# A gated linear recurrence with a SiLU feed-forward on one core: every engine's program order written anew, buffers in fixed rings, sine from the table set of SiLU

## The chip, the core and the metric

The kernel runs on one core of one Trainium2 chip. The metric is device time in microseconds (us). The kernel before took 656.92 us, the median of three runs (657.31, 653.33 and 656.92). The profile shown below is of one further execution, whose first-to-last-instruction span is 655.6 us.

## What is computed

Cut to what matters:

```python
B, H, S, D = 4, 8, 768, 48
mag = sqrt(a_re**2 + a_im**2); scale = minimum(mag, 0.999) / (mag + 1e-6)
a = scale * (a_re + 1j * a_im)                  # one complex gate per step and channel
for t in range(S):
    S_re, S_im = Re(a_t * S) + k_t v_t^T, Im(a_t * S)
    y_t = q_t . S_re
x = y.transpose(0, 2, 1, 3).reshape(3072, 384)
h = x @ w_in                                    # 384 x 2048
out = (h * sigmoid(h)) @ w_out                  # 2048 x 384
```

All is in 32-bit floats; the two weights arrive as 64-bit words and are turned into 32-bit floats on the chip.

## The kernel before, in words

The sequence of each of the four batch rows is cut into six chunks of 128 steps, which makes 24 tiles, n = 0 to 23. Two tiles are a pair p = n // 2, so there are 12 pairs. A tile of chunk c in row b needs the state that the tile four places earlier left.

**The recurrence of a tile.** The gates become a log-magnitude `l` and an angle `th` (squares, logarithm, exponential, arctangent on ScalarE, the arithmetic on VectorE). A matmul with a triangle of ones sums them over the 128 steps: `phases` (L453) and `sums` (L489). `turn` (L462) takes the angle down to one turn, `trig` (L473) takes sine and cosine, `decays` (L502) the exponentials, `rotated` (L530) makes the rotated keys and queries. They must stand transposed. For tiles 0 to 3 that is done by TensorE (`turned` L544, with the copies `placed` L575). From tile 4 on it is done by VectorE in 32 x 32 blocks (L566, the tile `sq`) and by twelve DMAs, six on SyncE's queue and six on GpSimd's (L571), which carry the blocks to their places in `T`. `weights` (L578) multiplies keys with queries (the tile `a`), VectorE masks the result (L595, the tile `w`), `output` (L598) makes `y`, `state` (L664) and `carried_on` (L703) the new state; from tile 6 on the state too is turned by VectorE and twelve small DMAs (L691, L699). ScalarE copies `y` to `xT` (L623, L627) and six small DMAs (L631) spread the last two heads.

**The feed-forward of a pair.** There are eight groups: `hidden` (L720) multiplies two 128-column blocks of `w_in` with the 256 tokens of `xT`, `silu` (L731) takes the activation on ScalarE into `g`, and `result` (L763) adds that group's part of the output. Pairs 0 and 1 use plain products (L773). Pairs 2 to 11 use seven products of half blocks for eight (L817), which need sums of `g` (`gs`, L760, VectorE) and sums of the weights (`wc`, L748). The last of the eight ends with a ScalarE copy, seven VectorE adds (L825, L829) and the store.

**The weights.** There are 28 blocks. `fetch` (L182) loads one, ScalarE takes the low words (`convert_low`, L224), VectorE the high words (L47, L49) and joins them (L56). `small` (L243) and `looked_at` (L255) reload all of the weights in 32 parts near the end of the program and look for values too small for this conversion; with the smallest decay of all tiles (L1062 to L1073) they make the value `weak`, which every engine loads before it branches around a slow spare path (L1075 and L1076). A tile of `small` takes a buffer of the gates `re` or `im`, two of each.

**Order.** Each engine works through its instructions in the order in which they are written. Up to pair 2 this order is a list of words (L1019 to L1043) that was written by hand, as in "h:0" for the next group of `hidden` of pair 0. From pair 3 on it is one string of marks, `usual` (L1048), that is repeated for each pair: the feed-forward of pair p - 1 is spread between the attention steps of pair p and the gates of pair p + 1. After the last attention step the looks at the weights (`look`, L884) are taken between the remaining groups. The code after these lists (L1057 on), among it the making of `weak`, is placed by the scheduler of the compiler. Buffers come from pools that hand out one of several buffers for each name. A sequence of ScalarE functions from different table sets needs a table load; the sets are natural logarithm with exponential, arctangent with sine, and SiLU. L300 is the explicit load of `table`; L305 is the line of `special`, at which the compiler adds loads of its own.

Of the kernel before, what the change touches and what calls it, by code (L numbers as in the profile page):

```python
# [11 lines left out]
F32 = mybir.dt.float32  # L12
# [45 lines left out]

@with_exitstack
def kernel(  # L60
# [44 lines left out]
    ld = fast.enter_context(tc.tile_pool(name="ld", bufs=2))  # L105
    pre = fast.enter_context(tc.tile_pool(name="pre", bufs=1))
    att = fast.enter_context(tc.tile_pool(name="att", bufs=2))
    moe = fast.enter_context(tc.tile_pool(name="moe", bufs=2))
    setup = ExitStack()
    su = setup.enter_context(tc.tile_pool(name="su", bufs=1))  # L110
    conversion = ExitStack()
    cv = conversion.enter_context(tc.tile_pool(name="cv", bufs=1, side="right"))
    later = {}
    startup_psum = ExitStack()
    p_m = fast.enter_context(tc.tile_pool(name="p_m", bufs=2, space=PSUM))
    p_h = fast.enter_context(tc.tile_pool(name="p_h", bufs=2, space=PSUM))
    p_o = startup_psum.enter_context(tc.tile_pool(name="p_o", bufs=4, space=PSUM))
# [20 lines left out]
    def load_a(p, queue=None):  # L138
        for name in ("re", "im"):
            A[p][name] = flat(pre.tile([C, 2, H, D], F32, tag=name, name=f"{name}{p}", bufs=2))  # L140
        for i in range(2):
            b, c = place(2 * p + i)
            for name, ap in (("re", a_re), ("im", a_im)):
                (queue or (nc.gpsimd if p == 0 and i and name == "re" else nc.sync)).dma_start(
                    out=cut(A[p][name], i).rearrange("p (h d) -> p h d", d=D),
                    in_=ap[b].rearrange("h (c p) d -> p c h d", p=C)[:, c])

    def load_x(n, names="kqv", queue=None):
        b, c = place(n)
        for name, ap in zip("kqv", (k, q, v)):  # L150
            if name not in names:
                continue
            if name == "v":

                X[n]["all v"] = ld.tile([C, DM + 64 - D], F32, tag="v", name=f"v{n}", bufs=4)
                nc.gpsimd.memset(X[n]["all v"][:, DM:], 0.0)
                X[n]["v"] = X[n]["all v"][:, 0:DM].rearrange("p (h d) -> p h d", d=D)
            else:
                X[n][name] = ld.tile([C, H, D], F32, tag=name, name=f"{name}{n}", bufs=2)
            (queue or nc.sync).dma_start(  # L160
                out=X[n][name], in_=ap[b].rearrange("h (c p) d -> p c h d", p=C)[:, c])
# [42 lines left out]
    def words(n):  # L204
        if n == len(fetched):
            fetch(1)
        dst, _, parts = blocks[n]
        return dst, fetched[n], parts[0][1].dtype != F32

    def convert_high(n):  # L210
        for _ in range(min(n, len(blocks) - len(highs))):
            dst, raw, does = words(len(highs))
            if does:
                high_part(nc, dst, raw[:, :, 1])
            highs.append(dst)

    def convert_low(n):

        for _ in range(n):
            dst, raw, does = words(len(lows))  # L220
            r = None
            if does:
                r = cv.tile([C, WC], I32, tag="wr", name="r", bufs=3)[:, 0:dst.shape[1]]
                nc.scalar.mul(r, raw[:, :, 0].bitcast(U32), 2.0 ** -29)  # L224
            lows.append(r)

    def convert(n):

        for _ in range(min(n, len(blocks) - len(done))):
            if len(done) == len(lows):  # L230
                convert_low(1)
            if len(done) == len(highs):
                convert_high(1)
            dst, r = highs[len(done)], lows[len(done)]
            if r is not None:
                joined(nc, dst, r)
            done.append(dst)

    def converted(which):
        while any(x[1] == which for x in blocks[len(done):]):  # L240
            convert(1)
# [32 lines left out]
    load_a(0)  # L274
# [10 lines left out]
    chained = []  # L285
    by_hand = []
    looks, looked = [], []

    def behind(ins, other):
        tc.add_manual_dep(ins.ins, other.ins.name, mybir.DependencyInfo(  # L290
            mybir.DependencyClass.NoSync, mybir.DependencyReason.DATA))

    def chain(ins):
        if chained and not by_hand:
            behind(ins, chained[-1])
        chained.append(ins)


    def table(of):
        chain(nc.scalar.preload_act_table_set({  # L300
            "exp": "natural_log_exp_and_others", "trig": "trig_and_small",
            "silu": "silu_and_others"}[of]))

    def special(out, in_, func, **kw):
        chain(nc.scalar.activation(out=out, in_=in_, func=func, **kw))  # L305


    def tiles(p, i):

        g = A[p]  # L310
        if "th" not in g:
            for x in ("s1", "s2", "mag"):
                g[x] = flat(pre.tile([C, 2, H, D], F32, tag="t3", name=f"{x}{p}", bufs=5))
            for x in ("l", "th"):
                pool = su if p == 1 else pre
                g[x] = flat(pool.tile([C, 2, H, D], F32, tag=x, name=f"{x}{p}"))
        names = ("re", "im", "s1", "s2", "mag", "l", "th")
        return (g[x] if i is None else cut(g[x], i) for x in names)
# [5 lines left out]
    def squares(p):  # L324
        re, im, s1, s2, _, _, th = tiles(p, None)
        special(s1, re, AF.Square)
        special(s2, im, AF.Square)
        special(th, re, AF.Abs)

    def gates_square(p):  # L330

        squares(p)
        magnitude(p)

    def magnitude(p):
        re, im, s1, s2, *_ = tiles(p, None)
# [3 lines left out]
    def gates_log(p):  # L340

        re, im, s1, s2, mag, *_ = tiles(p, None)
        special(s1, s1, AF.Ln)
        special(mag, s1, AF.Exp, scale=0.5)
        gates_excess(p)

    def gates_excess(p):
        re, im, s1, s2, *_ = tiles(p, None)
# [3 lines left out]

    def gates_inverse(p):

        re, im, s1, s2, mag, _, th = tiles(p, None)
        nc.vector.tensor_tensor(out=mag, in0=mag, in1=th, op=ALU.add)
        special(mag, mag, AF.Ln)
        special(mag, mag, AF.Exp, scale=-1.0)


    def early_square(i):
        re, im, s1, s2, _, _, th = tiles(0, i)
        special(s1, re, AF.Square)
# [5 lines left out]
    def early_log(i):  # L369

        re, im, s1, s2, mag, l, _ = tiles(0, i)
        special(s1, s1, AF.Ln)
        special(s2, s1, AF.Exp, scale=-0.5)
        nc.vector.tensor_scalar(out=l, in0=s1, scalar1=LN_CAP2, scalar2=0.5, op0=ALU.min,
                                op1=ALU.mult)

    def early_l(i):
        re, im, s1, s2, mag, l, th = tiles(0, i)
        special(s2, s2, AF.Ln, scale=1e-6, bias=one_b)
        nc.vector.tensor_tensor(out=l, in0=l, in1=s2, op=ALU.subtract)  # L380
        special(mag, s1, AF.Exp, scale=0.5)
        nc.vector.tensor_tensor(out=mag, in0=mag, in1=th, op=ALU.add)
        sums(i)

    def early_ratio(i):
        *_, mag, _, _ = tiles(0, i)
        special(mag, mag, AF.Ln)
        special(mag, mag, AF.Exp, scale=-1.0)
# [3 lines left out]
    def gates_l(p, i=None):  # L392

        re, im, s1, s2, mag, l, _ = tiles(p, i)
# [3 lines left out]
    def gates_ratio(p, i=None):  # L398

        re, im, s1, s2, mag, l, _ = tiles(p, i)  # L400
        nc.vector.tensor_tensor(out=mag, in0=mag, in1=im, op=ALU.mult)

    def gates_atan(p, i=None):
        re, im, s1, s2, mag, *_ = tiles(p, i)
        special(mag, mag, AF.Arctan)

    def gates_side(p, i=None):

        re, *_ = tiles(p, i)
# [3 lines left out]
    def gates_angle(p, i=None):  # L413

        re, im, s1, s2, r, l, th = tiles(p, i)
# [12 lines left out]
    def in_two(n, x):  # L428
# [3 lines left out]
        t = later["left"].tile([C, 2, DM], F32R, tag="part", name=f"{x}_parts{n}", bufs=2)  # L432
# [20 lines left out]
    def phases(n):  # L453
# [5 lines left out]
        if n >= STRAIGHT:  # L459
            turn(n)  # L460
# [12 lines left out]
    def trig(n):  # L473
# [8 lines left out]
        if n >= STRAIGHT:  # L482
            last_of(n)
# [5 lines left out]
    def sums(n):  # L489
# [7 lines left out]
        if not first:  # L497

            x["L"] = x["ek"]
            nc.vector.tensor_scalar(out=x["L"], in0=ps, scalar1=L_MIN, scalar2=None, op0=ALU.max)  # L500

    def decays(n):  # L502
# [6 lines left out]
        if not n < STRAIGHT:  # L509
            ends_of(n)  # L510
# [19 lines left out]
    def rotated(n, which="kq", hs=slice(None)):  # L530

        x = X[n]
        for w in which:
            if (w, "decayed") not in x:
                decayed(n, w)
# [8 lines left out]
    def turned(n, groups=range(4)):  # L544


# [3 lines left out]
        T = x["T"]  # L550
        if n < EARLY:
            for g in groups:
                w, hh = divmod(g, 2)
                ps = (p_o if n < 4 else p_m).tile([D2, HH, C], F32, tag="o" if n < 4 else "m",
                                                  name=f"tp{n}_{g}")
                for h in range(HH):
                    nc.tensor.transpose(
                        ps[:, h],
                        x["kq"[w] + "r"][:, hh * HH + h].rearrange("p c d -> p (c d)"), ident)
                x["T", g] = ps  # L560
                if n >= STRAIGHT:
                    placed(n, g)
        else:
            sq = later["left"].tile([C, NB, 2 * H, Q], F32, tag="sq", name=f"sq{n}", bufs=2)
            for i, w in enumerate("kq"):
                nc.vector.transpose(sq[:, :, ts(i, H)], x[w + "r"].rearrange(  # L566
# [668 lines left out]
```

## Time and profile before

| what | value |
|---|---|
| median of 3 runs | 656.92 us |
| span of the profiled execution | 655.6 us |
| TensorE matmul busy | 634.7 us, 97% of the span |
| VectorE busy | 468.4 us, 71% |
| ScalarE busy | 367.2 us, 56% |
| GpSimd busy | 213.8 us, 33% |
| mean granted TensorE clock | 0.994 |
| bytes moved by DMA | 73.28 MB |

TensorE appears as PE, VectorE as DVE, ScalarE as ACT, GpSimd as POOL, SyncE as SP. Busy time is the union of the instructions of an engine. A matmul of 32-bit floats appears as two records. One 12-record group of `h` takes 2.59 us from start to start, one 14-record group of `o` 2.28 us. From 161 us to 513 us the same pattern returns every 50.24 us, once for each pair.

### The profile page before, as it was taken

Reading aid. Unit: us, or ns where it says so; the run is one execution under the profiler, and the core shown is the slowest. Engines: PE = TensorE matmul, PEld = TensorE weight load, DVE = VectorE, ACT = ScalarE, POOL = GpSimd, SP = SyncE. Lnnn points to the kernel's source line nnn. Section 1 sums busy time; section 2 is a strip of 40 time slices with the busy share of each in tenths; the row PEclk is TensorE's granted clock in tenths of the full one; section 3 lists DMA queues with packets and bytes.
Section 4 is the critical chain, followed back from the end, with each engine's and each line's share of the span. In section 5 each row is a group of like instructions: output and inputs, shape, how many; then the busy total and the mean of one; then the engine's idle time right before and its main releaser. Section 6 shows DMA issues by size and latency. Waiting matters only on the chain.

```text
span 655.6 us, 11519 instructions
## 1 busy us (share of the span) xinstructions
PE 634.7 (97%) x4084; PEld 562.1 (86%) x4084; DVE 468.4 (71%) x1009; ACT 367.2 (56%) x537; POOL 213.8 (33%) x368
## 2 busy tenths in 40 slices
PE   5789999999999999999999999999999999998997
PEld 4668866777999999999999999999999999987997
DVE  5898379847975885885895894894894895864543
ACT  6798599796852852762762672672681681410110
POOL 7436000370342334334334334234244240140000
PEclk9899999999999999999999999999999999998999
DMA  9878465583393394394295296187187183678640
GB/s 168 173 189 171 113 178 126 117 134 86 47 153 49 61 146 62 56 139 73 47 141 79 41 135 91 35 122 109 31 125 110 32 116 56 201 160 226 204 141 27
DMA packets 183445, 73.28 MB, mean 112 GB/s; under 512 B 166224, under 2 KB 171816, under 8 KB 183384
## 3 DMA queue, kind: packets, MB, share of 16 engines
q1 hardware_dynamic: 168424, 50.79, 39.5%
q0 software_dynamic: 11648, 17.20, 17.1%
q10 hardware_dynamic: 3312, 4.52, 1.9%
q8 instruction: 33, 0.54, 0.4%
q14 instruction: 28, 0.23, 0.1%
HBM read 48.90 MB, written 4.79 MB: 82 GB/s over the span
## 4 chain that ended last, share of the span: by engine, by line
PE 80%; ACT 7%; DVE 5%; DMA 4%; SPq 2%; issue 1%; DVEq 0%; ACTq 0%
PE h L725 32%; PE o L817 27%; PE a L584 6%; PE y L614 3%; PE o L773 3%; PE y L617 3%; DMA raw<-in_moe_w_in_dram 2%; PE s L687 2%; ACT L305 2%; SPq L571 1%; PE phase L446 1%; ACT mag L305 1%; ACT s L305 1%; PE L L446 1%; DMA im<-in_a_im_dram 1%
## 5 line engine op out<-in xcount | busy, mean ns | idle before, releaser
L725 PE MATMUL h<-xT,w 128*128 128x256 f32 x1152 | 260.6, 380 | 0.0
L725 PEld LDWEIGHTS h<-xT,w 128*128 128x128 f32 x1152 | 216.4, 190 | 29.2
L305 ACT ACTIVATE g<-h 128x512 f32<-128x512 f32 x96 | 55.3, 596 | 140.3 <-PE h L725 133.2
L571 POOL DMA_DIRECT2D T<-sq x120 | 77.5, 653 | 71.9 <-issue 56.0
L517 POOL DMA_DIRECT2D dec<-ends x48 | 30.8, 648 | 154.9 <-DMA ends<-eq 154.9
L300 ACT ACT_TABLE_LOAD x62 | 79.5, 1283 | 2.0 <-PEq L1219 0.9
L817 PE MATMUL o<-w,gs 128*128 128x192 f32 x320 | 77.8, 326 | 0.0
L699 POOL DMA_DIRECT2D S<-ssq x84 | 45.8, 553 | 94.8 <-DVE ssq L691 56.5
L595 DVE TENSOR_TENSOR w<-a,upto_r 128x512 f32<-128x512 f32 x48 | 32.9, 687 | 53.5 <-PE a L584 53.5
L817 PE MATMUL o<-w,g 128*128 128x192 f32 x320 | 67.2, 332 | 0.0
L817 PE MATMUL o<-wc,gs 128*128 128x192 f32 x320 | 64.9, 326 | 0.0
L623 ACT COPY xT<-y 128x384 f32<-128x384 f32 x20 | 9.6, 478 | 98.1 <-PE y L617 98.1
L817 PEld LDWEIGHTS o<-w,g 128*128 128x128 f32 x320 | 54.0, 191 | 4.5 <-issue 2.0
L817 PEld LDWEIGHTS o<-w,gs 128*128 128x128 f32 x320 | 56.3, 190 | 0.0
L584 PEld LDWEIGHTS a<-T 96*128 96x128 f32 x384 | 49.4, 191 | 7.6 <-issue 3.5
L584 PE MATMUL a<-T 96*128 96x128 f32 x384 | 51.3, 276 | 3.7 <-DMA T<-sq 2.5
L817 PEld LDWEIGHTS o<-wc,gs 128*128 128x128 f32 x320 | 54.2, 190 | 0.0
L760 DVE TENSOR_TENSOR gs<-g 128x128 f32<-128x128 f32 x160 | 38.6, 283 | 20.4 <-PE o L817 13.9
L773 PE MATMUL o<-w,g 128*128 128x384 f32 x128 | 43.7, 489 | 0.8 <-ACT g L305 0.8
L817 PE MATMUL o<-wc,g 128*128 128x192 f32 x160 | 38.9, 326 | 0.0
L773 PEld LDWEIGHTS o<-w,g 128*128 128x128 f32 x128 | 23.8, 190 | 16.7 <-ACT g L305 1.8
L614 PE MATMUL y<-w,v 128*64 128x128 f32 x320 | 36.0, 287 | 0.0
(123 smaller groups left out, 987.3 us busy)
## 6 DMA issues: line engine op xcount, KB each, us to landing
T<-sq SPq DMA_DIRECT2D x120, 64.0 KB
T<-sq POOLq DMA_DIRECT2D x120, 64.0 KB, 4.1
raw<-in_moe_w_out_dram SPq DMA_DIRECT2D x16, 384.0 KB
small<-in_moe_w_in_dram SPq DMA_DIRECT2D x16, 384.0 KB
small<-in_moe_w_out_dram SPq DMA_DIRECT2D x16, 384.0 KB
raw<-in_moe_w_in_dram SPq DMA_DIRECT2D x24, 192.0 KB
out_dram<-ot ACTq DMA_DIRECT2D x23, 192.0 KB
im<-in_a_im_dram SPq DMA_DIRECT2D x16, 192.0 KB
```

The costliest lines, as they stand in the source:

```text
L300: chain(nc.scalar.preload_act_table_set({"exp": "natural_log_exp_and_others", "trig": "trig_and_small", "silu": "silu_and_others"}[of]))
L305: chain(nc.scalar.activation(out=out, in_=in_, func=func, **kw))
L517: nc.gpsimd.dma_start(out=x["dec"][a * D:(a + 1) * D], in_=ends[n].rearrange("(h d) -> d h", d=D))
L571: (nc.gpsimd if a % 2 else nc.sync).dma_start(out=to[ts(b, Q), :, a], in_=sq[ts(a, Q), b])
L584: nc.tensor.matmul(ps[:, h], lhsT=x["kT"][:, hh * HH + h], rhs=x["qT"][:, hh * HH + h], start=True, stop=True)
L595: nc.vector.tensor_tensor(out=x["w", hh], in0=x["a", hh], in1=upto.unsqueeze(1).to_broadcast([C, HH, C]), op=ALU.mult)
L614: nc.tensor.matmul(to, lhsT=v_[:, cols], rhs=x["w", h // HH][:, h % HH], start=True, stop=not carried)
L699: (nc.gpsimd if g % 2 else nc.sync).dma_start(out=to[ts(b, Q), r, :, e], in_=sq[ts(g, Q), :, b, 0:e.stop - e.start])
L725: nc.tensor.matmul(ps[:, ji], lhsT=w1[:, dc, ts(jp * 2 + ji, C)], rhs=A[p]["xT"][:, dc], start=(dc == 0), stop=(dc == ND - 1))
L760: nc.vector.tensor_tensor(out=t[:, i], in0=a, in1=b, op=op)
L773: nc.tensor.matmul(A[p]["o"][m].rearrange("p n c -> p (n c)"), lhsT=A[p]["g", jp][:, ji, ts(m, C)], rhs=w2[:, j], start=(j == 0), stop=(j ...
L817: nc.tensor.matmul(o[i], lhsT=a, rhs=b, start=(jp == 0 and i < 4), stop=(final and j == jp and i in ((5, 3, 6, 2) if p == NP - 1 else (4, ...
```

## The change

What is computed, and by which engine, stays. Three things differ.

1. *Order.* The hand-written list and the string `usual` are gone. One list of some 1,500 words now holds the whole program, to the last group of pair 11 and the last look. Its words are finer: `decayed`, `masked`, `floor`, `state_squared`, `state_homed`, `sums_of`, `put`, `third_of`, `finish` and others, which used to be called inside a larger step, are placed on their own. The weight conversion `F R H J` (fetch, low, high, join) takes one block a word. Loads say for themselves which queue they use (a trailing "g" is GpSimd's). Below, "w:6.1" stands for `weights` of tile 6, heads 4 to 7, "h:2.3" for group 3 of `hidden` of pair 2, "r" for `result`, "gs" for its sums, "of" for `finish`, "t", "T" for the transposes by TensorE and their copies, "tk", "tq", "td" for the transposes by VectorE and their DMAs, "m" for the mask, "sm" and "lk" for the reload of a part of the weights and the look at it.
2. *Buffers.* A class `Ring` gives every buffer of a pool its own tag and hands them out in turn.
3. *Tables.* `special` keeps track of the loaded set. A sine is taken from whichever of the arctangent's and SiLU's sets is loaded, and loads SiLU's when neither is.

The core of the diff:

```diff
+class Ring:
+    def __init__(self, pool, bufs):
+        self.pool, self.bufs, self.count = pool, bufs, {}
+    def tile(self, shape, dtype, *, name, tag=None, bufs=None):
+        tag, bufs = tag or name, bufs or self.bufs
+        k = self.count[tag] = self.count.get(tag, -1) + 1
+        return self.pool.tile(shape, dtype, tag=f"{tag}_{k % bufs}", name=name, bufs=1)
...
-    p_m = fast.enter_context(tc.tile_pool(name="p_m", bufs=2, space=PSUM))
+    p_m = Ring(fast.enter_context(tc.tile_pool(name="p_m", bufs=1, space=PSUM)), 2)
...
+    SETS = {"exp": ("natural_log_exp_and_others", (AF.Exp, AF.Ln)),
+            "trig": ("trig_and_small", (AF.Arctan, AF.Sin)),
+            "silu": ("silu_and_others", (AF.Silu, AF.Sin))}
+    CHOICE = {AF.Exp: "exp", AF.Ln: "exp", AF.Arctan: "trig", AF.Sin: "silu", AF.Silu: "silu"}
...
     def special(out, in_, func, **kw):
-        chain(nc.scalar.activation(out=out, in_=in_, func=func, **kw))
+        if func in CHOICE and (loaded[0] is None or func not in SETS[loaded[0]][1]):
+            table(CHOICE[func])
+        nc.scalar.activation(out=out, in_=in_, func=func, **kw)
...
-                table:exp k:1 q:0 warm:30 sq:0 ln:0 k:0 v:0 a:1 v:1 thirds:0 sq:1 l:0 ln:1 l:1 ratio:0
...
-    usual = ("c h E h kA qA h r tA D kB h L qB r F h tB wA wB r G h A X a0A th uA uB h a1A r sA h a0B yA "
-             "r a1B sB r pA yB pB mA S r mB r lA lB")
...
+                hold: re:0 e0:0 im:0 e1:0 e2:0 im:1 re:1g k:1g e3:0 F: e4:0 e6:0 e0:1 e1:1 e7:0
...
+                rk:3.0 s:3 J: J: floor:4 k:4g t:3.0 G3:2 s:2 g:0.3 H: R: g:0.2 t:3.1 R: G6:2 G9:2
+                S:3 carry:5 r:0.2 r:0.3 H: H: thirds:3 carry:4 F: H: J: J: R: F: R: J: J: h:0.4
...
+                phase:15 L:14 floor:14 exp:14 ends:14 h:5.6 turn:15 gs:5.5 dk:14 w:13.0 m:13.0
...
+                sm:1 gs:11.4 sm:30 lk:1 sm:15 lk:30 gs:11.5 lk:15 sm:7 h:11.6 g:11.6 sm:10 lk:10
+                lk:7 sm:23 sm:4 lk:4 r:11.4 sm:6 gs:11.6 sm:16 sm:13 lk:23 sm:21 g:11.7 r:11.5
+                gs:11.7 lk:6 lk:16 r:11.7 of:11 lk:13 lk:21
```

## The prediction

> **What bounds the kernel now.** I read the page's shares and slices first, then one table by stage, then the chain of waits where the table shows gaps, then the timeline of the end.
>
> ```profile
> span 655.6 us, 11519 instructions
> ...
> PE 634.7 (97%) x4084; PEld 562.1 (86%) x4084; DVE 468.4 (71%) x1009; ACT 367.2 (56%) x537; POOL 213.8 (33%) x368
> ...
> PE   5789999999999999999999999999999999998997
> ```
>
> TensorE is the bound. No other engine comes above 71%, and the PE row has holes only in its first three digits and its last four. The same by stage (start:end, length, then busy us of PE, PEld, DVE, ACT, POOL, granted clock, DMA share, GB/s):
>
> ```profile
> 46.00:161.20 115.20, 113.72 (x610) 86.01 (x609) 81.53 (x144) 94.37 (x128) 32.02 (x47) 1.00 0.61 134
> 161.20:561.00 399.80, 399.80 (x2721) 369.93 (x2720) 301.92 (x663) 221.54 (x323) 142.90 (x252) 1.00 0.57 87
> 561.00:612.50 51.50, 48.98 (x306) 44.96 (x305) 30.19 (x75) 10.81 (x19) 11.79 (x19) 0.97 0.68 179
> 612.50:655.60 43.10, 38.90 (x208) 36.12 (x207) 19.96 (x64) 5.11 (x10) 0.00 (x0) 0.99 0.40 135
> ```
>
> For 400 us in the middle PE never idles: 399.80 of 399.80. A new order can't remove waits there, since there are none. It can change only how many PE instructions start a group[...], and it can add waits. What an order may win is before 161 us and after 561 us. The chain of waits (start, length, what) shows the hole near the end:
>
> ```profile
> 579.33 4.95 DMA small<-in_moe_w_in_dram
> ...
> 584.30 0.04 DVE tiny L257
> ...
> 584.77 1.84 DVE sq L566 x2
> ...
> 590.78 4.27 DMA T<-sq
> 595.05 0.39 issue
> 595.44 1.13 PE a L584 x8
> ```
>
> A reloaded part of the weights lands at 584.28. The look at it (L257) stands ahead of the sq transposes on VectorE; these stand ahead of six issues on SyncE (586.67 to 590.74, 4.1 us), whose transfer lands at 595.05. PE waited 0.56 us at 583.3 and 2.3 us until 595.44, and then its eight `y` groups took 3.27 us instead of the 1.96 of the steady part (+1.3), with 0.3 more on `o`. Together 4.5 us. The end, on VectorE:
>
> ```profile
> 634.34 0.19 DVE L1067 TENSOR_REDUCE fit<-tiny 128x1 f32<-128x32 f32 x1
> 634.57 0.15 DVE L1068 TENSOR_SCALAR fit<-fit 128x1 f32<-128x1 f32 x1
> 636.73 0.30 DVE L1073 TENSOR_REDUCE weak<-all__5772 1x1 int32<-1x152 f32 x1 [2.01 <-DMA all__5772<-fit]
> ```
>
> `weak` is ready at 637, while PE works to 651.4: the whole check is hidden. What follows the last matmul is 4.2 us, to 655.6.
>
> **What the Trainium skill says.** "PSUM — Partial Sum Buffer", section "Engine vs sequencer instructions": the queues of VectorE, ScalarE and GpSimd are strict FIFO, and matmuls complete in program order. The trace agrees: the look held back transposes whose inputs were ready, for the 4.95 us of its load. So with a written order each place in the list is a bet on when inputs come. "TensorE: Matmul & The Clock Gate", section "What's actually happening": the clock halves after an idle window of about 3.4 us. Here `y` slowed from 0.22 to 0.43 us per four records after an idle of only 2.3 us; the measurement decides, and a stall costs more than itself. "ScalarE: Activation LUTs", section "What ACT_TABLE_LOAD costs": 1283 ns and a drain of 1380 ns. The page's rows show 62 + 22 loads at 1283 ns, and a following activation starts 0.02 us after a load ends (16.92 after 15.62 + 1.28); the drain isn't seen.
>
> **The change part by part**, against the profiled execution's 655.6 us, which stands 1.3 us under the median of the runs.
>
> *Arithmetic.* Nothing is added or removed on PE, VectorE, GpSimd or in bytes. Table loads, counted in both instruction streams, are 84 before and 85 after: letting the sine use SiLU's set saves none, since the new order puts other functions between. Cost 1 x 1.28 us on ScalarE, hidden under its 44% idle time: 0 (if that cover were gone, 1.3).
>
> *Start, to y:5.* The first 51 us hold little choice: operands arrive by DMA. I walked the new PE order by hand with the durations of the trace: y:0 at 36.8 us as before, the first `h` at 45.4 (before 46.0), the first pair of `h` done at 50.6 (51.3). From there to the end of y:5 PE has 96.4 us of work; packed without a gap it would end at 147.0. Before, the same work ends at 152.1 (161.2 less the 9.1 us which before does there beyond y:5). Against packing stands VectorE's and ScalarE's weight conversion: 28 blocks, 12 x 1.84 + 16 x 1.46 = 45 us on VectorE, which before spreads to about 150 us and the new list puts ahead of r:0.6, at about 95 us. The walk gives waits of 0.7 (h:0.6), 1.5 (r:0.6) and 1.6 us (the copies and masks of tile 3), and smaller ones: y:5 ends at 151.6. **−0.5 us** (from −4.6 with no wait to +4 if conversion is twice as late as in my walk).
>
> *Middle.* PE's groups keep their durations, but a switch to `y` or `s` makes the next group slower: `o` takes 2.47 us after `y` and 2.28 otherwise, `h` 2.79 after `s` and 2.59 otherwise. So 0.2 us a visit. After y:5 before makes 32 such visits, and the new list, which sets most `y` of a pair side by side and `s` beside them, 19: 13 x 0.2 = **−2.6 us** (0 to −3).
> Where before has no stall, a stall may come. Three places: (a) from `td` (VectorE's transposes and their twelve DMAs) to the `a` that reads T, the new PE order leaves 9.4 to 10 us for tiles 8 to 10 and 22. Needed are six issues of 0.65 = 3.9 to 4.1, and a landing of 4.1: 8.0 to 8.5. A margin of 1 us; single issues are seen to take 1.4 to 1.8 us. Each issue counts on its queue: on SyncE the carried-state, `xT`, load and store DMAs stand between, on GpSimd its own six and the loads marked "g". (b) The two PSUM buffers for `m` and `x` go in a fixed turn, 0 to 0.5 us each. (c) Every item that a td, m or w waits for holds back all that is behind it on VectorE, gs and masks first, and `r` waits for gs. From the walk I take **+2.0** for all (0 to 8).
> VectorE has 132 us of single instructions before y:5, which at its overlap of 0.907 (union 468 of a sum of 517) is 120 in 151; ScalarE 122. Neither takes over as bound.
>
> *Tail stall.* The new list has all reload parts near the last two tiles placed where their issues don't hold SyncE ahead of T's. The 4.5 us goes: **−4.5** (0 if only moved).
> What is late next: four parts can be in flight, each landing 4.3 to 4.95 us after issue, and 27 looks now stand in the last 49 us on VectorE between the `gs`. gs:11.1, gs:11.6 and gs:11.7 stand behind looks, and r:11.7 behind these: **+1.0** (0 to 3).
>
> *Epilogue.* The list ends "r:11.7 of:11 lk:13 lk:21"; VectorE's stream has the two looks, fit (L1067), its comparison and weak (L1073) behind the last adds of the output. Before, all of these are done 14 us ahead of the last matmul. Now, from the last matmul T: adds to T+0.4 for the first and the rest behind, two looks 1.0, then fit 0.19 + 0.15, the DMA of all_ and weak, 2.74 from the end of the looks to SyncE's load, load and branch 0.6 and more: T+7.9 instead of T+4.2. **+3.7** (the cover that is gone is the last 14 us of matmuls; +2 if looks and adds overlap better, +5 if the last part's load lands late).
>
> Sum: 655.6 − 0.5 − 2.6 + 2.0 − 4.5 + 1.0 + 3.7 = 654.7; on the median's scale + 1.3 = **656.0 us**.
>
> **The rivals.** *Faster.* The order packs the start (−4.6 for −0.5), and neither the middle nor the last looks stall (−3): 656.0 − 4.1 − 3.0 = 648.9, with a start better by another 1 to 2 us still 647. For it: PE has 1.5 to 4.6 us of gaps there and the other engines 20% room. Against it: VectorE and ScalarE are at their busiest just there (94 of 115 us), with conversion earlier by 50 us.
> *Slower.* T lands after its `a`. Place: the td of tiles 8 to 10 and following, on the SyncE and GpSimd queues. Price: issue queue later by 2 us against a margin of 1 gives a stall of about 1 to 2.1 us, and `y` behind it at the slow clock 1.3 and 0.3: up to 3.7 us a tile. It passes 1% from the third such tile (3 x 3.7 = 11): **667**. For it: single issues up to 1.8 us, and the same stall in before's own tail. Against it: the pattern of before runs 50.24 us a pair without one.
> *The change doesn't do what it says.* Sine from SiLU's table saves no load (85 for 84). I hold that likely in itself; the time stays 656.0.
>
> **How the numbers follow.** Likeliest, gains and losses within 1%: 0.67, at 656.0, own range 650 to 662. Faster rival 0.13, slower rival 0.20. About 1% (650.4 to 663.5) is what a measurement of this kernel can tell from no change. The range 648 to 666 takes in the likeliest's bounds, most of the faster rival and the near half of the slower.
>
> **What would show it.** Right: y:5 ends near 151.6; PE's gaps after it sum to 1 to 4 us; no wait for T at the last tiles; last matmul near 647 and some 8 us behind it, with `weak` after the last adds; 85 table loads. Wrong: waits of `a` for T over 2 us at several tiles (slower), or a PE busy share of 99% and y:5 at 147 to 148 (faster). Should the weak check be hidden after all, 3.7 us goes.

## The result, and the profile after

The changed kernel takes 664.73 us (median of four runs, 662.14 to 666.06), the kernel before in the same comparison 657.12 us. The ratio is 1.0137, 95% interval 1.0092 to 1.0182: slower, where the prediction was 656.0 us and no change over 1%.

The page of the changed kernel, the same parts as before (TensorE was 97%, 634.7 us; its row had its holes at both ends):

```profile
span 660.4 us, 11615 instructions
...
PE 631.6 (96%) x4084; PEld 559.0 (85%) x4084; DVE 469.5 (71%) x1009; ACT 370.6 (56%) x538; POOL 212.9 (32%) x368
...
PE   6599999999999999999998999999999999999995
```

PE is busy 3.1 us less in a span 4.8 us longer. The hole near the end has gone; the last digit has fallen to 5. By stage (columns as before; 154.75 us is the end of y:5), and then the first 46 us of the kernel before:

```profile
0.00:46.00 46.00, 31.85 (x240) 24.35 (x240) 35.43 (x68) 38.55 (x59) 26.73 (x50) 0.89 0.87 178
...
154.75:561.00 406.25, 401.87 (x2729) 369.60 (x2728) 294.86 (x648) 237.50 (x332) 143.53 (x255) 1.00 0.51 86
561.00:612.50 51.50, 51.37 (x333) 47.90 (x332) 29.30 (x77) 8.10 (x17) 10.51 (x17) 1.00 0.43 88
```

```profile
0.00:20.00 20.00, 11.67 (x71) 8.11 (x72) 11.04 (x24) 11.76 (x22) 12.76 (x28) 1.00 0.91 174
20.00:46.00 26.00, 21.64 (x175) 16.93 (x175) 23.74 (x43) 23.62 (x38) 14.38 (x22) 0.93 0.75 176
```

The middle, 399.80 of 399.80 before, now has 4.4 us without a matmul. The stretch from 561 us has 0.13 us where it had 2.5. And in the first 46 us PE is at work for 31.85 us, where it was 33.31 (11.67 + 21.64), at a mean granted clock of 0.89, where it was 0.96.

*The start.* The chain of waits (start, length, what) from 6.6 to 21 us:

```profile
6.58 10.38 DMA raw<-in_moe_w_in_dram
...
17.16 0.44 DVE w L47
...
19.28 0.57 DVE th L409
...
19.90 1.66 PE phase L434 x2
```

The second "H:" of the new list (L47, L49: high words of weight block 1) stands on VectorE ahead of the gates of tiles 0 and 1. Its block takes 10.4 us to land. VectorE stood still for 3.21 us (the number in brackets is the idle time before an instruction):

```profile
17.16 0.43 DVE L47 TENSOR_SCALAR w<-raw 128x512 int32<-128x512 int32 x1 [3.21 <-DMA raw<-in_moe_w_in_dram]
```

phase:0, which needs three more instructions of VectorE, starts at 19.90 us.

*The body.* These lines of PE's list of waits (what waited, for what, us in total, times, longest) hold its three largest waits behind y:5, and the only waits of `a` for a DMA:

```profile
PE y L596 <- DVE w L577: 1.6, 1, 1.6
PE h L711 <- DMA xT<-y: 1.0, 1, 1.0
...
PE o L803 <- DVE ot L816: 0.8, 1, 0.8
...
PE a L569 <- DMA S<-ssq: 0.2, 1, 0.2
```

The first, near 345 us, in SyncE's queue (SPq) and then in the chain:

```profile
331.36 5.59 SPq L557 DMA_DIRECT2D T<-sq  x6
...
339.90 3.82 SPq L685 DMA_DIRECT2D S<-ssq  x6
343.76 0.59 SPq L169 DMA_DIRECT2D k<-in_k_dram  x1
```

```profile
343.76 3.26 DMA k<-in_k_dram
...
347.12 0.10 DVE L L512
...
347.59 0.68 DVE w L577
```

The load of k:14 is issued behind six issues for T, two loads of re and six for S. dk:14 (L512) waits for it 2.84 us on VectorE, and behind dk:14 stand the masks of tiles 12 and 13 (L577). PE pays at its next `y`, the 1.6 us of the list: 64 records that take 3.86 us elsewhere take 5.57. The second, near 411 us:

```profile
411.59 5.78 DMA xT<-y
...
417.50 0.67 PE h L711 x2
```

The six small DMAs of pair 7 are issued behind loads of re, im, v and the carried rows, and `h` waits for them. PE idles 1.0 us; against the usual time of its groups it loses 1.4. The third, at 481 us, 0.8 us idle and 1.1 lost, comes from carried:21, which waited 2.83 us on VectorE for `carry`.

*The end.*

```profile
643.54 9.11 PE o L803 x56
...
653.03 0.93 DVE tiny L252 x2
...
654.39 1.98 DMA all__5790<-fit
...
656.39 0.30 DVE weak L1016
```

The last matmul ends at 643.54 + 9.11 = 652.65 us (before: 651.4), and 7.75 us follow it (before: 4.2): the last adds of the output, two looks (L252), and fit with its DMA and weak.

So the profiled execution's 4.8 us are 1.25 us to the end of PE's work and 3.55 us in the tail.

### The profile page after: what moved, and what is told of

Same layout as the page of the kernel before. It is cut to its first block, busy times and chain, and to the rows that moved or that the text cites. A ratio compares the mean times of both kernels' runs of the same rounds, so it can differ in the third digit from the quotient of the medians.

```text
span 660.4 us, 11615 instructions
## 1 busy us (share of the span) xinstructions
PE 631.6 (96%) x4084; PEld 559.0 (85%) x4084; DVE 469.5 (71%) x1009; ACT 370.6 (56%) x538; POOL 212.9 (32%) x368
## 4 chain that ended last, share of the span: by engine, by line
PE 70%; DVE 10%; DMA 8%; ACT 5%; SPq 3%; issue 2%; POOL 0%; DVEq 0%; ACTq 0%
PE h L711 29%; PE o L803 22%; PE a L569 5%; DMA raw<-in_moe_w_in_dram 4%; PE o L756 4%; PE y L596 3%; PE y L599 2%; SPq L557 2%; ACT s L292 1%; DMA im<-in_a_im_dram 1%; ACT L286 1%; PE s L667 1%; DVE ot L816 1%; DMA xT<-y 1%; DVE gs L742 1%
## 5 line engine op out<-in xcount | busy, mean ns | idle before, releaser
L577 DVE TENSOR_TENSOR w<-a,upto_r 128x512 f32<-128x512 f32 x48 | 32.7, 685 | 46.7 <-PE a L569 33.7
L685 POOL DMA_DIRECT2D S<-ssq x84 | 45.9, 554 | 26.3 <-DVE ssq L674 12.9
L292 ACT ACTIVATE cs<-turn 128x384 f32<-128x384 f32 x46 | 21.6, 516 | 29.9 <-DVE turn L457 19.4
```

The lines of the kernel that those rows point to most:

```text
L577: nc.vector.tensor_tensor(out=x["w", hh], in0=x["a", hh], in1=upto.unsqueeze(1).to_broadcast([C, HH, C]), op=ALU.mult)
L685: (nc.gpsimd if g % 2 else nc.sync).dma_start(out=to[ts(b, Q), r, :, e], in_=sq[ts(g, Q), :, b, 0:e.stop - e.start])
```

## The experiments

Ratios are to the kernel before on the same chip. Its own median was 654.6 to 657.1 us in these comparisons, so ratios are compared, not medians. In brackets behind a ratio stands its 95% interval. Of each profile I also use three points of PE: the first `h`, the end of y:5 and the end of the last matmul.

**The changed kernel once more.**

> The changed kernel as it is, once more, as the reference for the edits sent with it. Expected 664 us (662 to 666), about 1.3% above the kernel before. In its profile: VectorE waits about 3 us near 14 us for a weight block (raw), the first h starts near 48 us, and 7.8 us pass between the end of the last matmul and the end of the program. If the other executions of this kernel (664 to 666) lose their time in another place than the first profile shows, this profile tells where.

Measured: 666.03 us, ratio 1.0156 (1.0111 to 1.0201). Its profiled execution has a span of 664.7: first h at 49.4 us (48.0 in the first profile), end of y:5 at 158.35 (154.75), from there to PE's end 498.6 (497.9), tail 7.8. The first profile was of the quickest of four runs. What this execution loses beyond it lies ahead of y:5: VectorE waits 4.39 us for the weight block instead of 3.21, and 2.2 us more are lost between the first `h` and y:5. For the changed kernel below I take the mean of the two ratios, 1.0146. Each has an interval of 0.0045 to either side, so by my estimate a difference of less than some 0.004 (2.5 us) between two ratios is not told apart, and rests on the profiles alone.

**H late.** The second H moved; nothing else.

```diff
-im:2g H: q:1g at:0.0 k:0g e5:1 im:3g H: q:0g e6:1 ... phase:0 re:3g dq:1 e7:1 dk:1 e8:1 turn:0
+im:2g H: q:1g at:0.0 k:0g e5:1 im:3g q:0g e6:1 ... phase:0 re:3g dq:1 e7:1 dk:1 e8:1 H: turn:0
```

> The changed kernel with only the second H (the high words of weight block 1, on VectorE) moved from before the excess of tile 1 to just before turn:0. Theory (this H waits 3.2 us for its block to land, and the first phases, y:0 and the first h stand behind it): phase:0 at 16 to 17 us for 19.9, first h at 45 to 46 us for 48.0, time 2 to 3 us less, about 661.5. Rival (VectorE has no idle time from 17 to 50 us, so its sum of work sets the first h): first h at 47.5 or later and no measurable difference, 664.

Measured: 660.17 us, ratio 1.0092 (1.0056 to 1.0127). PE's timeline (start, length, instruction, and in brackets the idle time before it):

```profile
15.63 0.91 PE L434 MATMUL phase<-th,upto_r 128*128 128x384 f32 x2 [0.61 <-DVE th L409]
22.25 1.65 PE L434 MATMUL phase<-th,upto_r 128*128 128x384 f32 x2 [5.71 <-DVE th L409]
```

phase:0 comes at 15.63 for 19.90 us; first h at 44.9, end of y:5 at 152.07. The rival, that VectorE's sum of work sets the first h, falls: of the 3.2 us of waiting, 3.1 come back at the first h, and 4.5 against the second profile of the unrepaired kernel, whose wait was 4.4. Phase:0 too is quicker, 0.91 us for 1.66. 1.0146 − 1.0092 = 0.0054, about 3.5 us.

**Looks spread.** 30 of the 32 reloads between 555 and 632 us, three of every seven in the buffers `t3` that the gates have left, and the making of `weak` in words of the list ahead of r:11.7 (z0 and z1: the smallest decay, z2: fit and its DMA, z3: weak).

```diff
-    raw = pre.tile(..., tag=("re", "im")[n % 2], name=f"small{n}", bufs=2)
+    raw = pre.tile(..., tag=PLACE[n], name=f"small{n}", bufs=5 if PLACE[n] == "t3" else 2)
...
-gs:11.7 lk:6 lk:16 r:11.7 of:11 lk:13 lk:21
+r:11.1 r:11.2 lk:29 lk:30 lk:31 z2: ... gs:11.4 z3: ... gs:11.7 r:11.7 of:11
```

> The changed kernel with only the reload of the weights and its looks moved: 30 of the 32 parts are loaded and looked at between 555 and 632 us, three of seven in buffers that the gates have left free, and the value weak is made before the last group of pair 11. Theory (the check of the weights lies bare behind the last matmul and costs 3.6 us): the tail behind the last matmul falls from 7.8 to about 4.2 us and the time by 3.5 us, to about 660.5. Rival (what is late is in the body, and the looks when put earlier hold VectorE up in front of gs and masks): the tail falls, but PE ends as much later, time 663 to 665.

Measured: 663.76 us, ratio 1.0131 (1.0092 to 1.0170). The tail fell to 4.25 us as expected, and I had put the reloads badly (SyncE's queue, then the chain):

```profile
558.24 1.78 SPq L247 DMA_DIRECT2D small<-in_moe_w_in_dram  x4
560.06 0.43 SPq L169 DMA_DIRECT2D k<-in_k_dram  x1
```

```profile
560.06 6.74 DMA k<-in_k_dram
...
566.81 0.56 DVE L L514
```

Four reloads stood on SyncE ahead of the load of k:23. The first of them waited 12.9 us for a buffer that a look had still to free, and k:23 behind it left the queue at 560.06 us; in the next kernel, with the reloads behind it, it leaves at 545.29. It then took 6.74 us to land for the 3.26 us of k:14 above. dk:23 held VectorE up for 6.64 us, gs behind it, and `o` 2.0 us. So both the theory and its rival were right here. In the changed kernel two reloads stand ahead of k:23, and SyncE waits 12.9 us there too. With these four placed behind the load and the small DMAs of pair 10:

> The changed kernel with only the looks spread, the first four reloads behind the load of k:23 as in the combined kernels. Theory (bare check 3.6 us): tail 4.2 us, 661.5, ratio about 1.010. Rival (the reloads take back part of it elsewhere, as the small gain in the combined kernel's median suggests): 663 to 664.

Measured: 662.00 us, ratio 1.0112 (1.0092 to 1.0132), tail 4.2 us; 1.0146 − 1.0112 = 0.0034, 2.2 us, which the intervals alone do not tell from none. The tail's 3.6 us are plain in the profile, and the other 1.4 us are in part seen: this kernel has two waits of 0.5 us that the changed one has not. At 605 us three looks (1.38 us) stand on VectorE ahead of S:18, for which `y` waits; at 617 us `h` waits for small DMAs behind reloads on SyncE.

**Three body words** (four words, at three places). k:14 ahead of the S DMAs of tile 13, xd:7 directly behind x:15, carried:21 and carry:23 behind of:7.

```diff
-h:5.5 im:17 ut:14 ... sd:13 S:10 g:5.5 k:14 r:5.2
+h:5.5 k:14 im:17 ut:14 ... sd:13 S:10 g:5.5 r:5.2
...
-x:14 x:15 s:15 ... gs:6.7 xd:7 tk:17
+x:14 x:15 xd:7 s:15 ... gs:6.7 tk:17
...
-last:19 carried:21 carry:23 h:8.3 ... of:7 re:22
+last:19 h:8.3 ... of:7 carried:21 carry:23 re:22
```

> The changed kernel with only the three body words moved (k:14, xd:7, carried:21 with carry:23). Theory (these waits cost 3 to 4.5 us by themselves): 661 to 662, ratio to the kernel before about 1.010, with the waits near 350, 412 and 481 us gone and the start and the tail as in the changed kernel. Rival (their gain with the other repairs came from those): 664 to 666.

Measured: 659.76 us, ratio 1.0081 (1.0062 to 1.0099); 0.0065, 4.3 us. The queue that held k:14:

```profile
331.25 0.39 SPq L169 DMA_DIRECT2D k<-in_k_dram  x1
...
342.42 3.82 SPq L685 DMA_DIRECT2D S<-ssq  x6
```

The load is out 11 us before S's DMAs. PE's stretch from the end of y:5 to its last matmul is 494.1 us, for 497.9 and 498.6 in the two profiles of the changed kernel. None of the three waits came back elsewhere.

**The repairs together.** First H late with the looks spread:

> The changed kernel with the second H late and the looks spread, the first four reloads now placed behind the six small DMAs of pair 10 and so behind the load of k:23 on SyncE. Theory (two prices that add up: the bare check of 3.6 us and the wait of H of 4 to 5 us): tail 4.2 us, first h at 45 us, no wait of o at 565 us, time 3.6 us under the kernel with H alone late, 656.5, about 0.4% above the kernel before. Rival (the reloads collide with the loads of the last tiles wherever they stand): time 658 to 661, with new waits between 560 and 620 us.

Measured: 659.10 us, ratio 1.0062 (1.0047 to 1.0078). Only 0.003 (2 us) under H late alone, too little for the intervals: the tail is 4.1, but PE's part behind y:5 is 0.8 us longer, with the same two waits of 0.5 us, at 600 and 611 us. That is the rival's time and place; the price of the bare check stands (tail 8.0 us with H alone late and 4.1 here), the repair gives part of it back. With the three body words:

> As the last one, and in addition three words moved in the body: the load of k:14 ahead of the S DMAs of tile 13, the small DMAs of pair 7 (xd:7) to just behind x:15, and carried:21 with carry:23 behind the adds of pair 7. Theory (each is a VectorE or PE instruction that waits for a DMA which is queued late on SyncE; lost are 1.7 and 0.4 us near 350, 1.4 near 412, 1.1 near 481 us): these waits go and the time is 2 to 3.5 us less than the last kernel, about 654. Rival (the slack is only passed on to the next DMA on the same queue): gain under 1 us, with waits at other places of the same stretches.

Measured: 654.40 us, ratio 0.9984 (0.9969 to 0.9999). From the changed kernel that is 0.0162, 10.6 us; the three repairs by themselves give 3.5 + 2.2 + 4.3 = 10.0. Within the intervals they add up. With the looks moved off S:18 and the small DMAs of pair 11 ahead of the reloads:

> The changed kernel with all repairs (H late, looks spread, three body words moved) and two more at the end: no looks ahead of S:18, and the small DMAs of pair 11 ahead of the last reloads on SyncE. Theory: the 0.5 us of y at 597 us and the 0.5 us of h at 608 us go, time 1 us less than the kernel with the three body words moved, 653.5. Rival: no difference, 654.4. Against the kernel before with looks apart, 651.5, it stays behind if the start and the body still hold 2 us of waits for DMAs, which I expect.

Measured: 653.45 us, ratio 0.9967 (0.9955 to 0.9979). The two waits are gone from the profile; the gain by the ratio, 0.0017 or 1.1 us, is the expected one but within the intervals.

**The table rule undone.** The same order, but a sine always in the arctangent's set.

```diff
-            "silu": ("silu_and_others", (AF.Silu, AF.Sin))}
-    CHOICE = {..., AF.Sin: "silu", AF.Silu: "silu"}
+            "silu": ("silu_and_others", (AF.Silu,))}
+    CHOICE = {..., AF.Sin: "trig", AF.Silu: "silu"}
```

> The changed kernel with only the table rule undone: a sine always uses the set of the arctangent. In this order that makes 112 table loads for 84, 28 x 1.28 = 36 us more on ScalarE, which is idle 44% of the time. Theory (ScalarE has the room, the table part of the change is worth nothing by itself): 664 to 666, no measurable difference. Rival (a load stands between the h of a group and its silu, or ahead of the copies of y, so that r or h waits): several loads come through to PE, 0.3 to 1 us each, 670 to 680.

Measured: 684.87 us, ratio 1.0460 (1.0408 to 1.0512): 20 us slower than the changed kernel, more than even the rival said. The loads are 112 x 1.283 us. Near 592 us the chain shows how a load gets from an engine that is busy 60% of the time to PE:

```profile
591.88 1.28 ACT L286
...
594.77 1.28 ACT L286
...
596.07 0.61 ACT g L292
...
596.72 4.85 PE o L803 x14
```

Two loads around three sines stand ahead of the silu that `o` waits for. This one wait costs 5.25 us: PE idles 2.72 us, and then the 14 records of `o` take 4.85 us for the 2.28 they take elsewhere, at a granted clock of 0.50. With SiLU's set the same place costs 0.4.

**The kernel before, looks apart.**

```diff
+            if x in ("tA", "tB") and p + 1 == NP:
+                apart = x == "tA"
-            if x in "hr" and p + 1 >= NP:
+            if x in "hr" and p + 1 >= NP and not apart:
...
-        for _ in range(1 + (len(looks) % 6 == 0)):
+        for _ in range(1 + (len(looks) % 4 == 0)):
```

> The kernel before with only its looks moved: none between the transposes of tile 22 and those of tile 23, and one more after every fourth instead of every sixth. Theory (the wait for T near 595 us and the slow matmuls after it cost 4.5 us, all through the look in front of the transposes): no wait of a for T at tile 23, PE busy 98% from 561 to 612, time 4 to 4.5 us less, about 652.5 (ratio 0.993). Rival (the wait moves to the next look or to the masks, or the later looks lay the check bare): 655 to 658.

Measured: 651.46 us, ratio 0.9955 (0.9941 to 0.9969). The stretch that had 48.98 us of PE in 51.50:

```profile
561.00:606.00 45.00, 45.00 (x297) 41.95 (x296) 28.26 (x69) 10.51 (x18) 11.74 (x19) 1.00 0.68 167
```

The stall is gone, and in the profile PE's part behind y:5 is 4.6 us shorter. The ratio gives only 2.0 to 3.9 us. The profile of the kernel before is a slow one: wherever a run has both numbers, device time is 1.7 us above the span (651.4 for 649.7 here), so by estimate its 655.6 us stand for 657.3, which is 2.5 above its median of 654.75 over 24 executions in this comparison, while this kernel's profile stands at its median (651.4 for 651.46). Of that excess, 1.25 us lie ahead of y:5, which ends at 156.10 us in the one profile and at 154.85 in the other. So in a usual execution the stall is worth some 3 us and not 4.5; no second profile of the kernel before shows it.

**The same, with the y of a pair side by side.**

```diff
-"... h a1A r sA h a0B yA r a1B sB r pA yB pB mA S ..."
+"... h a1A r sA h a0B r a1B yA yB sB r pA pB mA S ..."
```

> The kernel before with its looks apart from the transposes and, from pair 3 on, one thing of the new order: the two y of a pair stand side by side, with s of the second tile behind them (a1B yA yB sB, for yA, r, a1B, sB, r, yB). Theory (each group of o or h that follows y, s or a phase is 0.2 us slower, and this arrangement makes one to two fewer such switches in each of nine pairs): the 50.24 us of a pair falls by 0.2 to 0.45 us, the time by 2 to 4 us against the kernel with the looks apart, to about 649. Rival (the second y must wait for its mask, whose buffer the first y frees only as it ends): the pair takes 50.3 to 51 us and the time is 651 to 656.

Measured: 647.47 us, ratio 0.9880 (0.9856 to 0.9903), and this version beats both kernels. A pair now takes 49.66 us for 50.24. The chain of the kernel with the looks apart, and then of this one (`a`, the `y` and the second `o` are left out):

```profile
245.61 2.47 PE o L817 x14
...
248.98 0.81 PE s L687 x16
...
252.26 0.35 PE phase L446 x2
...
254.58 0.55 PE phase L446 x2
255.13 4.55 PE o L817 x28
```

```profile
243.23 2.28 PE o L817 x14
...
250.25 0.66 PE s L687 x16
...
253.39 0.70 PE phase L446 x4
254.09 4.58 PE o L817 x28
```

The two `phase` groups have come to stand side by side as well. The first `o` takes 2.28 for 2.47 us, both `y` 3.85 for 3.92, `s` 0.66 for 0.81, both phases 0.70 for 0.90, and the pair of `o` 4.58 for 4.55: 0.58 us a pair, 5.2 in nine pairs. The ratio fell by 0.0075, 4.9 us. It was more than expected because I had counted `o` and `h` alone: in these chains a short group behind another short one is cheaper too, as `s` behind `y` shows.

## Why the prediction was wrong, and where it was right

Against the profiled execution, forecast 654.7, measured 660.4; the median was forecast at 656.0 and measured at 664.73. That lies in the wide range of 648 to 666, but outside the 650 to 662 of the outcome held likeliest, gains and losses that cancel. Three steps failed: the start, where a wait was put at nothing; the waits behind y:5, which were put too low; and the step from a profile to the median. Their misses, 3.15, 2.7 and 3.0 us, less 0.15 in the tail, are the 8.7 us by which the median was missed.

| step | forecast, us | measured, us |
|---|---|---|
| start, to the end of y:5 | 151.6 | 154.75 |
| y:5 to the last matmul's end | 495.2 | 497.9 |
| tail | 7.9 | 7.75 |
| from this to the median of the runs | 1.3 | 4.3 |

*The start: wrong.* "The walk gives waits of 0.7 (h:0.6), 1.5 (r:0.6) and 1.6 us": the walk gave every instruction its duration and looked at conversions as work. In the first 20 us, the part that I said holds "little choice" because operands arrive by DMA, I did not ask when the raw block of the second H would be there. That wait stood at nothing in the sum. The block came at 17 us, after 10.4 us, and cost 3.1 us at the first h in the profiled execution and 4.5 in the second profile. H late shows it. Beyond it the walk came out well: with H late y:5 ends at 152.07 for 151.6.

*The middle: mechanism right, size wrong.* Item (c) named it, a word on VectorE that waits and all that is behind it. I gave +2.0 for (a), (b) and (c) and +1.0 for the last looks, 3.0. Each PE group's time less the usual time for its shape and predecessor adds up to 5.7 us after y:5. The three body words alone are worth about 4.3 us by their ratio. The term was mis-sized by 2.7 us, because I took margins for T only, and PE never waited for T: its waits hold none of `a` for T. Late were transfers that stood on SyncE behind other issues: k:14, the small DMAs of pair 7, a carried row.

*The slower rival* gave the right sign with the wrong mechanism. It put the loss at T of tiles 8 to 10.

*Fewer switches: right.* 651.4 − 152.1 − 4.5 = 494.8 us of work before, 497.9 − 5.7 = 492.2 after: −2.6, as predicted. The count of 13 holds too: behind y:5 the profile before has 33 stretches of `y` and `s`, that after has 20, if a `y` and an `s` side by side are taken as one. No run takes the new arrangement alone out of the new list; that such an arrangement gains is shown on the kernel before, by the pair with its y side by side.

*Tail stall and epilogue: right.* −4.5: 51.37 us of 51.50 are busy where it was, though the 4.5 us are those of a slow execution (above). The looks bring the tail from 4.2 to 7.75, +3.55 for +3.7, and back to 4.2 when spread. The prediction's "586.67 to 590.74" are five of the six issues; the sixth starts at 590.78, and nothing in the sum changes. As a place to gain, the 3.55 us is worth less: of the spread looks, 1 us or more comes back as waits on SyncE and VectorE.

*The table: wrong.* "Letting the sine use SiLU's set saves none" compared 85 loads with 84. The right comparison was with the new order under the old rule, 113 by the same count (112 of `table` and one of the compiler). The rule is what lets that order put sines between silus, and is worth 20 us in it. No number of the sum hung on this, and so the forecast didn't suffer.

*From profile to median: wrong.* I added 1.3 us, as for the kernel before. It was 4.3. Of this, 1.7 us is the distance of device time from the span (662.14 for 660.4), and 2.6 comes from profiling the quickest of four runs; for the kernel before, the 1.3 was the same 1.7 less 0.4, since its profiled execution was not a quick one. The second profile of the changed kernel puts 3.6 of its 4.3 us more ahead of y:5: 1.4 are there at the first `h`, behind the weight block, and 2.2 come between it and y:5, with 1.3 in one wait of `o` for `g`.

In all, the new order brought −2.6 (switches) and −4.5 (stall), and gave back 3.55 (tail), some 3 to 4.5 (the weight block) and 4 to 6 (loads behind other issues). The old order with two edits has both gains and none of these losses.

What stays open: why the load of that block takes 10 us, since nothing was run on the order of the first loads (from 10 to 20 us the DMA engines' busy share is 1.04, 0.98 in the kernel before, so that the block waits for them is likely, and not shown); how long the stall of the kernel before is in a usual execution; and what the rings are worth, since every kernel of the new order has them and none was run without.

## What to carry to other kernels

When an order is written out, ask of every word that consumes a DMA when its issue leaves its queue and what that queue issues first, not only how long the word takes. Such a word holds all behind it on its engine, and in this case words at three places among 1,500 cost 4 us. The queue holds as well: a load that waits for its buffer keeps back those behind it, here k:23. Check what stands behind the last matmul, and judge a rule that enables an order against that order without it.

## What was not expected of the hardware

A load of one tile of k landed 3.26 us after its issue near 344 us, and 6.74 us behind four reloads of 384 KB each on the same queue. A weight block in the first 17 us took 10.38 us, and 11.52 in the second profile. And two `phase` groups of the same size took 0.91 and 1.65 us in one execution (H late): the second came after PE had waited 5.71 us. The Trainium skill, "TensorE: Matmul & The Clock Gate", section "What's actually happening", says that the clock halves after an idle window of about 3.4 us; 1.65 / 0.91 = 1.8, and a granted clock of 0.50 from 22 to 26 us, agree with it here. Shorter idle times did it too: with the table rule undone the clock stood at 0.50 from 596 to 602 us, after PE had idled for 2.72 us.
